# A linear-attention and gated-FFN kernel on one core: another way of bringing in the first weights and heads of k, and another order of the steps

## The chip, the core and the metric

The kernel runs on one core of a Trainium2 chip. It drives five engines that each take their instructions in order: TensorE (PE; its weight loads are listed apart as PEld), VectorE (DVE), ScalarE (ACT), GpSimd (POOL) and SyncE (SP). Transfers between memory and the core are started by SP, ACT or POOL and carried out by 16 DMA engines. The metric is the device time of one execution in microseconds; the median of several runs is given, with the lowest and highest.

## The reference

Attention with a feature map in place of the softmax, on 8 batches of 8 heads, 576 tokens and 64 dimensions, and a gated FFN on its output:

```python
def phi(x):                                    # w_phi: 64 x 128
    proj = np.einsum('bhsd,df->bhsf', x, w_phi)
    proj = proj - np.max(np.abs(proj), axis=-1, keepdims=True)
    return np.concatenate([np.exp(proj), np.exp(-proj)], axis=-1)
q_p, k_p = (phi(q), phi(k))
kv = np.einsum('bhsf,bhsd->bhfd', k_p, v)
z = np.sum(k_p, axis=2)
num = np.einsum('bhsf,bhfd->bhsd', q_p, kv)
den = np.einsum('bhsf,bhf->bhs', q_p, z)[..., None] + 1e-06
x = (num / den)                                # then 4608 tokens x 512
out = (np.maximum(x @ w_gate, 0.0) * (x @ w_val)) @ w_out   # 512 -> 1536 -> 512
```

## The kernel before

Everything is written as small steps, and one string, ORDER (from line 16), lists all 2041 of them in the order in which they are issued. Each word is a step: `ke.0.1.2.0:3@kp0` calls `do_ke` with the arguments 0, 1, 2, 0 (batch 0, head group 1, chunk 2, sign 0), the PSUM bank 3, and buffer 0 of the ring kp. The engines take their own instructions from this list in order, so a step that waits holds back all later steps of its engine. Waits between engines follow from the tiles that are read and written; there are eight PSUM banks.

Each batch has heads in three groups (0 and 1; 2 to 4; 5 to 7) and four chunks of 128 tokens, and 64 more tokens per head apart. The steps that matter here:

- Loads. `lk` (k, line 417), `lq` (q, line 424), `lm` (the 64 last tokens of k, lines 431 and 436), `lv` of batch 0 (v, line 454), `wl` (w_gate and w_val, line 477) and `wo` go by POOL, which casts fp32 to bf16 on the way where the tile is bf16. `wp` (line 373) and `wq` (line 379) bring w_phi in fp32 by SP: w32f holds four copies on 32 partitions each, w64f two copies on 64. `lv` of later batches (line 459), `lw` (the last tokens of v, line 469) and `gt` (line 466, one element of k read into a tile `mark`, behind which the next loads of SP wait until k has landed) go by SP.
- `wc` and `wd` cast w32f and w64f to bf16 on DVE (lines 382, 385). `ms` are memsets on DVE, `id` and `if` the identity on POOL and its fp32 copy on DVE.
- `zz.n` are n matmuls of zeros with zeros into a bank (line 408): filler that computes nothing.
- k of batch 0: `k0` transposes a head group on PE (line 533), `k1` copies it to kT on DVE (line 536), `k2` projects it with w64 (line 554). Later batches use `kt` (a DVE transpose, line 495) and `kr` (projection with w32, line 511). Then `ke` takes exponentials on ACT (line 563), `kx` maxima on DVE (line 571), `kk` and `kp` the scale factors on ACT (lines 580, 591), and `vs`, `vd`, `vr`, `vo`, `vp` scale v with them on POOL (lines 618, 637, 630) and DVE (lines 600, 608). `kv` multiplies features with v on PE (line 658), `kc` or `kd` copies it out (line 669).
- q: `qt` transposes on DVE (line 685), `qs` or `qc` projects with w32 on PE (line 694), `qe` exponentials on ACT (line 709), `qx` maxima on DVE (line 717), `qy`, `qz`, `qu`, `qw` the scale (lines 727, 735, 743, 750). `nu` multiplies with kv on PE (line 757); `nt`, `nv`, `nr` combine on DVE (lines 778, 788, 796); `nx` normalizes on POOL (line 800); `xp` with `xa` or `xc`, or a DMA transpose `xt` (line 817), puts the result into xT.
- FFN: group g takes the tokens of batch g, group 8 the last tokens of all. `fv` and `fg` (line 916; in group 0 partly by quarters, `pv` and `pg`, line 945) fill a bank, `va` (ACT, line 931) or `vb` (DVE, line 934) copies the value half out, `ga` (DVE, line 937) gates; `fo` (line 977) multiplies with w_out, `oc` (ACT) or `oe` (DVE) copies out, `od` stores by SP. The very last tile is done in two halves (`fp`, `o1`, `o2`, `d1` by ACT, `d2` by SP).

xT of group 8 has a tile of its own, xTm (`xT_mix`), 128 x 4 x 512 bf16, which is first written by the transposes of group 8, the first of them after the last tokens of batches 0 and 1 are done.

Of the kernel before, what the change touches and what calls it, by code (L numbers as in the profile page):

```python
# [8 lines left out]
FP32 = mybir.dt.float32  # L9
# [12 lines left out]
qt.0.0@qT1 kx.0.2.3:7 ke.0.2.2.1:6 kx.0.2.2:6 kx.0.0.0:2@mk2 lv.0.1 ke.0.0.2.1:1@kp2 ke.0.2.1.0:5  # L22
lm.1.0 lv.0.0 ke.0.0.3.1:3 ke.0.0.1.0:0 ke.0.2.0.0:4 lv.0.2 ke.0.0.0.1:2 kk.0.1.0 lm.1.1 wl.1.0
kx.0.2.1:5 kp.0.2.1:7 ke.0.0.0.0:2 ke.0.2.0.1:4 lw.0.1 qs.0.1.0:6 kx.0.0.1:0 kx.0.0.3:3 qx.0.1.0:6
vs.0.1.1@vs0 kp.0.2.0:7 qs.0.0.1:5 qe.0.0.1.0:5@qp0 gt.0 lk.1.3 qs.0.0.2:2 lv.1.2 kx.0.0.2:1
ke.0.2.3.0:7 vp.2:7@vs1 kk.0.0.1@ek1 vs.0.1.0 ke.0.0.2.0:1 qs.0.0.0:4 wl.0.1 kk.0.0.0 ke.0.0.3.0:3
qx.0.0.0:4 qx.0.0.2:2 vo.0@vs2 vd.0.2.0:7 ke.0.0.1.1:0 qs.0.1.1:1 qe.0.0.1.1:5 qe.0.0.0.1:4@qp1
qx.0.1.1:1 qs.0.1.2:3 qe.0.1.2.0:3@qp2 qe.0.0.0.0:4 qs.0.0.3:0 qe.0.0.3.0:0@qp3 wl.0.0 qe.0.1.0.0:6
qs.0.1.3:4 qx.0.0.1:5 qe.0.0.3.1:0 vd.0.2.1:7 qe.0.1.0.1:6 qe.0.1.1.0:1 vr.0.0.0 vr.0.0.1 qy.0.0:5
qx.0.1.2:3 vr.0.1.0 qx.0.1.3:4 vr.0.1.1 kv.0.2:7 kc.0.2:7@kv0 vo.1 kv.0.1:6 qz.0.0:5@my0 qu.0.0@mz0  # L30
qw.0.0@cq0 qx.0.0.3:0 kt.1.1@kT0 nu.0.0.2:7 nt.0.0.2:7@t0 qe.0.1.3.1:4 qy.0.1:0 qz.0.1:0@my0
vs.0.0.1 kc.0.1:6 ku.1@kT1 vs.0.0.0 kv.0.0:5 qe.0.1.3.0:4 nu.0.0.1:6 nt.0.0.1:6@t1 kc.0.0:5
qe.0.0.2.0:2 qu.0.1@mz0 qw.0.1 qy.0.2:0 qe.0.1.1.1:1 nv.0.0.1:6@u0 qe.0.1.2.1:3 qy.0.3:4 nu.0.0.0:5
nt.0.0.0:5@t2 qe.0.0.2.1:2 nv.0.0.2:7 nv.0.0.0:5 nr.0.0@r0 nu.0.1.1:1 qz.0.2:0@my0 qu.0.2@mz0 lv.1.0
# [12 lines left out]
qe.1.1.1.0:4 kr.1.0:2573 ke.1.0.1.1:5@kp0 ke.1.0.3.1:3 ke.1.0.2.1:7 ke.1.0.0.0:2 ke.1.0.3.0:3
pv.1.2:4 qt.1.0@qT0 kx.1.0.1:5@mk2 lw.1.1 pa.1.2:4@val1 ke.1.0.0.1:2 nx.0.3@xu1 xp.0.3:6 xc.0.3:6
kx.1.0.2:7 wl.1.2 pg.1.2:0 pb.1.0:1 ke.1.0.2.0:7 ke.1.0.1.0:5 kx.1.0.3:3 pv.0.3:6 pa.0.3:6@val0
fv.0.8:4 va.0.8:4@val2 ln.0.1 qc.1.0:5371 wo.2 pv.1.3:6 vs.1.1.0 kx.1.0.0:2 kk.1.0.0@ek0 kk.1.0.1  # L50
qe.1.0.1.1:3 vr.1.0.1 vs.1.0.0@vs0 pb.1.2:0 qx.1.0.2:7 qx.1.0.0:5 kt.1.2@kT1 qe.1.0.2.1:7
qe.1.0.3.0:1 qe.1.0.0.0:5 vr.1.1.0 qe.1.0.2.0:7 ms.1 pc.1.3:6@val1 pg.0.3:4 pb.0.3:4 qx.1.0.3:1
fv.0.10:0 va.0.10:0@val3 fv.0.11:2 lk.2.3 qe.1.0.0.1:5 va.0.11:2@val0 qx.1.0.1:3 kr.1.2:0476
kx.1.2.0:0@mk2 ke.1.2.3.0:6@kp1 pg.1.3:5 fg.0.11:2 kx.1.2.2:7 kx.1.2.3:6 qe.1.0.1.0:3 ke.1.2.1.1:4
kx.1.2.1:4 ke.1.2.2.0:7 qe.1.0.3.1:1 ku.2@kT1 ke.1.2.0.1:0 pb.1.3:5 kk.1.2.0@ek2 ke.1.2.2.1:7
fv.0.9:3 va.0.9:3@val1 fg.0.8:1 ke.1.2.1.0:4 wo.1 lv.2.3 ga.0.11:2 vr.1.0.0 qy.1.0:7 qz.1.0:7@my0
mt.0 fg.0.10:5 ga.0.8:1 kk.1.2.1 ke.1.2.0.0:0 vs.1.0.1 mc.0:4732 me.0.2.0:3 mx.0.3:2 me.0.0.0:4
qu.1.0@mz0 mx.0.2:3 me.0.0.1:4 vr.1.1.1 vo.1.0 kv.1.0:0 kc.1.0:0@kv1 ga.0.10:5 mx.0.0:4 qw.1.0@cq0
mx.0.1:7 vs.1.1.1 kv.1.1:1 me.0.2.1:3 kc.1.1:1 nu.1.1.0:0 nt.1.1.0:0@t2 fg.0.9:5 vo.1.2@vs1 lv.2.0
kt.2.1@kT0 vs.1.2.1 nu.1.0.0:1 me.0.3.1:2 ga.0.9:5 ke.1.2.3.1:6 nu.1.0.1:4 nu.1.1.1:3 nt.1.1.1:3@t0  # L60
nt.1.0.0:1@t1 vs.1.2.0 kv.1.2:6 nv.1.1.0:0@u0 nv.1.1.1:3 me.0.1.0:7 kt.2.0 lw.2.1 fo.0.1.0:5
kc.1.2:6 nu.1.0.2:6 nt.1.0.2:6@t0 nu.1.1.2:3 nt.1.0.1:4@t2 me.0.3.0:2 nu.1.2.0:2 nt.1.2.0:2@t3
nv.1.0.0:1@u1 me.0.1.1:7 lq.2.2 nv.1.0.2:6 nv.1.0.1:4 nr.1.0@r0 nv.1.2.0:2@u2 fo.0.1.1:5 fo.0.1.2:5
oc.0.1:5@ob0 nt.1.1.2:3@t2 nu.1.2.2:4 nt.1.2.2:4@t3 lw.2.0 nv.1.1.2:3 nr.1.1@r1 kr.2.0:2617
ke.2.0.0.0:2@kp0 kx.2.0.3:7@mk2 lv.2.1 ke.2.0.0.1:2 od.0.1 nu.1.2.1:0 nt.1.2.1:0@t2 nx.1.0@xu1
kx.2.0.2:1 ke.2.0.1.1:6 kx.2.0.0:2 nu.1.3.2:5 nt.1.3.2:5@t0 nv.1.2.1:0 ke.2.0.3.1:7 fo.0.0.0:3
fo.0.0.1:3 nv.1.3.2:5@u1 xt.1.0 fo.0.0.2:3 nu.1.3.0:5 ke.2.0.2.1:1 nv.1.2.2:4 nr.1.2@r0
nt.1.3.0:5@t3 nx.1.1@xu0 nu.1.3.1:0 nt.1.3.1:0@t0 nv.1.3.0:5 nv.1.3.1:0 nr.1.3@r1 ke.2.0.3.0:7
ke.2.0.2.0:1 oc.0.0:3@ob0 ke.2.0.1.0:6 kt.2.2@kT1 nx.1.2@xu2 kr.2.1:4172 ke.2.1.2.0:7@kp1 kx.2.0.1:6
fo.0.2.0:3 fo.0.2.1:3 ke.2.1.1.1:1 xt.1.1 ke.2.1.0.1:4 ke.2.1.3.1:2 fo.0.3.0:0 ke.2.1.0.0:4  # L70
# [190 lines left out]
def kernel(  # L261
# [17 lines left out]
    C = 4  # L279
# [787 lines left out]
```

## Time and profile before

| | |
|---|---|
| median of 3 runs | 378.97 us (378.84 to 379.15) |
| profiled execution | 378.79 us, of which the span of the profile is 376.8 us |
| PE busy | 367.3 us, 97% of the span |
| DVE busy | 296.3 us, 79% |
| ACT busy | 222.6 us, 59% |
| POOL busy | 161.4 us, 43% |
| memory read and written | 37.95 MB and 9.44 MB, 126 GB/s over the span |

A profile is one execution taken by the hardware profiler; its span is 2.0 us shorter than the time of that execution. Several views of it are used. The slices divide the span into 40 equal parts and give the busy share of each engine in tenths, and the granted clock of PE (PEclk) in tenths of full speed. The table of stages gives busy microseconds and the number of instructions of each engine in stretches that one chooses. The chain of waits follows the last instruction back, step by step, to what released it. The timeline lists instructions in order of time with the idle time before them. Matmul ends are modelled, so a busy PE is not yet a PE at its peak; the distance from one matmul's start to the next tells more.

### The profile page before, as it was taken

Reading aid. Unit: us, or ns where it says so; the run is one execution under the profiler, and the core shown is the slowest. Engines: PE = TensorE matmul, PEld = TensorE weight load, DVE = VectorE, ACT = ScalarE, POOL = GpSimd, SP = SyncE. Lnnn points to the kernel's source line nnn. Section 1 sums busy time; section 2 is a strip of 40 time slices with the busy share of each in tenths; the row PEclk is TensorE's granted clock in tenths of the full one; section 3 lists DMA queues with packets and bytes.
Section 4 is the critical chain, followed back from the end, with each engine's and each line's share of the span. In section 5 each row is a group of like instructions: output and inputs, shape, how many; then the busy total and the mean of one; then the engine's idle time right before and its main releaser. Section 6 shows DMA issues by size and latency. Waiting matters only on the chain.

```text
span 376.8 us, 9181 instructions
## 1 busy us (share of the span) xinstructions
PE 367.3 (97%) x3591; PEld 197.2 (52%) x3591; DVE 296.3 (79%) x680; ACT 222.6 (59%) x539; POOL 161.4 (43%) x180
## 2 busy tenths in 40 slices
PE   8788999999999999999999999999999999999996
PEld 6457857546544645455435554464444644444443
DVE  3989999989996899989989898888876657642351
ACT  1988996998578544776586547755774400302111
POOL 7777595595477042581475233812341212200000
PEclk9859999999999999999999999999999999999999
DMA  9999999699954664289713944193400021301122
GB/s 126 235 200 220 148 176 152 112 129 143 122 118 58 147 72 113 57 138 91 103 64 37 189 120 99 35 155 92 86 28 3 2 70 57 91 22 29 28 57 111
DMA packets 90513, 38.04 MB, mean 101 GB/s; under 512 B 64230, under 2 KB 85734, under 8 KB 90470
## 3 DMA queue, kind: packets, MB, share of 16 engines
q0 software_dynamic: 33904, 15.23, 31.2%
q1 hardware_dynamic: 56422, 22.10, 27.7%
q8 instruction: 28, 0.46, 0.6%
q10 hardware_dynamic: 144, 0.13, 0.1%
q14 instruction: 15, 0.12, 0.1%
HBM read 37.95 MB, written 9.44 MB: 126 GB/s over the span
## 4 chain that ended last, share of the span: by engine, by line
PE 89%; DVE 5%; ACT 4%; DMA 2%; issue 0%; SPq 0%; DVEq 0%; ACTq 0%
PE bank L916 46%; PE bank L977 22%; PE bank L658 6%; PE bank L757 4%; PE bank L945 4%; PE bank L694 3%; ACT kp L563 2%; PE bank L511 2%; DMA w64f<-in_w_phi_dram 2%; DVE mk L571 1%; ACT qp L709 1%; PE bank L1006 1%; PE bank L898 1%; DVE u L788 1%; DVE maxq L717 1%; DVE t L778 1%
## 5 line engine op out<-in xcount | busy, mean ns | idle before, releaser
L563 ACT ACTIVATE kp<-bank 128x384 bf16<-128x384 f32 x192 | 83.2, 513 | 26.2 <-PE bank L511 15.0
L977 PE MATMUL bank<-wo,h 128*128 128x512 bf16 x420 | 98.3, 379 | 0.0
L937 DVE SCALAR_TENSOR_TENSOR h<-bank,val 128x512 bf16<-128x512 f32 x100 | 66.3, 681 | 29.8 <-PE bank L916 25.5
L916 PE MATMUL bank<-xTs,wg 128*128 128x512 bf16 x352 | 86.7, 379 | 0.0
L916 PE MATMUL bank<-xTs,wv 128*128 128x512 bf16 x352 | 86.2, 379 | 0.0
L800 POOL TENSOR_TENSOR xu<-u,r 128x512 bf16<-128x512 f32 x36 | 37.5, 1044 | 97.3 <-DVE r L796 92.4
L931 ACT CAST val<-bank 128x512 bf16<-128x512 f32 x70 | 41.6, 606 | 62.2 <-PE bank L916 50.8
L709 ACT ACTIVATE qp<-bank 128x512 bf16<-128x512 f32 x128 | 70.9, 632 | 10.1 <-DVE maxq L717 5.1
L618 POOL TENSOR_TENSOR vs<-vn,ek 128x780 bf16<-128x780 f32 (+3 forms) x40 | 53.0, 1338 | 37.8 <-ACT ek L580 35.1
L977 PEld LDWEIGHTS <-h 128*128 128x128 bf16 x420 | 39.1, 98 | 44.0 <-issue 0.9
L916 PEld LDWEIGHTS <-wv 128*128 128x128 bf16 x400 | 37.0, 98 | 43.2 <-issue 3.5
L916 PEld LDWEIGHTS <-wg 128*128 128x128 bf16 x400 | 37.4, 98 | 42.0 <-issue 1.8
L571 DVE TENSOR_REDUCE mk<-bank 128x3 f32<-128x384 f32 x96 | 49.0, 539 | 4.3 <-ACT kp L563 2.2
L717 DVE TRANSPOSE_TENSOR_REDUCE maxq<-bank 128x16 f32<-128x512 f32 x64 | 42.3, 692 | 3.5 <-PE bank L694 2.3
L986 ACT COPY ob<-bank 128x512 f32<-128x512 f32 x23 | 13.6, 593 | 37.5 <-PE bank L977 37.2
L788 DVE TENSOR_TENSOR u<-bank,t 128x195 f32<-128x195 f32 (+1 forms) x108 | 33.4, 330 | 1.9
L778 DVE TENSOR_TENSOR t<-bank,cq 128x195 f32<-128x195 f32 (+1 forms) x96 | 29.8, 327 | 5.0 <-PE bank L757 4.1
L757 PEld LDWEIGHTS <-qp 128*128 128x128 bf16 x512 | 24.1, 98 | 13.6 <-issue 2.0
L757 PE MATMUL bank<-kv,qp 128*128 128x65 bf16 x512 | 27.2, 194 | 1.2 <-ACT qp L709 0.8
L934 DVE CAST val<-bank 128x512 bf16<-128x512 f32 x30 | 20.2, 678 | 8.4 <-PE bank L916 8.3
L658 PEld LDWEIGHTS <-kp 128*128 128x128 bf16 x640 | 24.0, 101 | 3.7 <-DVE h L937 0.3
L658 PE MATMUL bank<-vs,kp 128*128 128x65 bf16 x512 | 24.2, 199 | 0.0
(88 smaller groups left out, 357.0 us busy)
## 6 DMA issues: line engine op xcount, KB each, us to landing
out_dram<-ob SPq DMA_DIRECT2D x31, 256.0 KB, 2.2
vn<-in_v_dram SPq DMA_DIRECT2D x24, 256.0 KB, 5.4
kn<-in_k_dram POOLq DMA_DIRECT2D x7, 512.0 KB, 6.4
qn<-in_q_dram POOLq DMA_DIRECT2D x7, 512.0 KB, 7.6
wg<-in_moe_w_gate_dram POOLq DMA_DIRECT2D x3, 512.0 KB, 8.5
wv<-in_moe_w_val_dram POOLq DMA_DIRECT2D x3, 512.0 KB, 10.0
wo<-in_moe_w_out_dram POOLq DMA_DIRECT2D x3, 512.0 KB, 8.7
out_dram<-ob SPq DMA_DIRECT2D x9, 128.0 KB, 2.4
```

Of the source, the lines that this page charges most:

```text
L563: nc.scalar.activation(kp_of(3 * b + j)[:, i, s].rearrange("p n f -> p (n f)"), bank[bk[0]][:, 0 : 3 * F], AF.Exp, scale=(1.0, -1.0)[s],)
L571: nc.vector.tensor_reduce(mk_of(3 * b + j)[:, :, i], bank[bk[0]][:, 0 : 3 * F].rearrange("p (n f) -> p n f", f=F), axis=AX.X, op=ALU.max, ...
L618: nc.gpsimd.tensor_tensor(vs_of(3 * b + j)[:, s, 0:n].rearrange("p n i e -> p (n i) e")[:, :, 0:e], src[:, lo:hi].rearrange("p h i e -> p ...
L658: nc.tensor.matmul(out_ps[:, h - lo, s, :], lhsT=lhsT, rhs=rhs, start=(at == 0), stop=(at == 2 * n * (C + 1) - 1),)
L709: nc.scalar.activation(qp_of(4 * b + i)[:, s, 4 * hq : 4 * hq + 4].rearrange("p h m -> p (h m)"), bank[bk[0]], AF.Exp, scale=(1.0, -1.0)[s],)
L717: nc.vector.tensor_reduce(maxq[:, :, i, 4 * hq : 4 * hq + 4].rearrange("p t h -> p h t"), bank[bk[0]].rearrange("p (h t u) -> p h t u", h= ...
L757: nc.tensor.matmul(bank[bk[0]][:, E * n : E * (n + 1)], lhsT=qp_of(4 * b + i)[:, s, h, :], rhs=kv_of(b)[:, h, s, :],)
L800: eng.tensor_tensor(xu_of(n).rearrange("p (h d) -> p h d", d=D), u_of(n)[:, :, 0:D], r_of(n).to_broadcast([P, H, D]), op=ALU.mult,)
L916: nc.tensor.matmul(bank[bk[0]], lhsT=w[:, dc, P * f : P * f + P], rhs=xT(g)[:, dc, :], start=(dc == 0), stop=(dc == NDC - 1),)
L931: nc.scalar.copy(val_of(NFC * g + f), bank[bk[0]])
L937: nc.vector.scalar_tensor_tensor(h2_of(g, f), bank[bk[0]], 0.0, val_of(NFC * g + f), op0=ALU.max, op1=ALU.mult)
L977: nc.tensor.matmul(bank[bk[0]], lhsT=h2_of(g, f)[:, P * t : P * t + P], rhs=wo_sb[:, f, :], start=(f == 0), stop=(f == NFC - 1),)
```

## The change

The first load of k (heads 2 to 4 of batch 0, `lk.0.1`) is no longer done by POOL with a cast on the way. It goes by SP in fp32 (`lf`), as the first transfer of SP's queue, into the memory of xTm, seen as fp32; two casts then write bf16 k on chip, heads 2 and 3 on DVE (`cf.0`) and head 4 on ACT (`cg.1`). w_phi for 32 rows (`wp`) is second in SP's queue. w_phi for 64 rows is brought by ACT (`wr` in place of `wq`) as ACT's first instruction.

ORDER is another one throughout, with 2053 words. POOL now builds the identity first and then loads k of heads 5 to 7, k of heads 0 and 1, and q of heads 4 to 7. The filler is cut into 15 pieces (before 5): 16 matmuls on bank 0, then twelve pieces of 2 to 8 on bank 1, the last of them just ahead of `kv.0.2`, then 3 and 2 on bank 3 around the first `xp`; 79 filler matmuls in all (before 62). `wc` comes after the first maxima of k. Of the steps that may run on two engines, a few change: `oc` 22 and `oe` 13 (before 23 and 12), `va` 69 and `vb` 31 (before 70 and 30), `pa` 8 and `pc` none (before 7 and 1). All other kinds of steps are there as often as before.

```diff
 ORDER = """
-ms.0 ms.2 ms.3@vr0 lk.0.1 ms.6 wp wq ms.4@vr1 wd ms.5 lq.0.1 wc id if zz.37:0 k0.1:0 k1.1:0@kT0
-zz.5:1 k2.1:0123 lk.0.2 ke.0.1.1.0:1@kp0 ke.0.1.2.0:2 ke.0.1.3.0:3 ke.0.1.0.0:0 qt.0.1@qT0
-ke.0.1.3.1:3 kx.0.1.1:1@mk0 lk.0.0 kx.0.1.2:2 ke.0.1.2.1:2 ke.0.1.1.1:1 lm.0.1 zz.6:4 k0.2:4
-k1.2:4@kT0 zz.7:5 k2.2:4567 ke.0.2.2.0:6@kp1 kx.0.1.3:3 ke.0.2.3.1:7 lm.0.0 lq.0.0 kx.0.1.0:0
-kx.0.2.0:4@mk1 ke.0.1.0.1:0 lw.0.0 k0.0:2 k1.0:2@kT0 zz.7:1 k2.0:2013 kk.0.1.1@ek0 ke.0.2.1.1:5
...
-tail: fp.7.2.0:4 oc.7.3:6@ob2 od.7.3 o2.7.2:7@ob0 d2.7.2 o1.7.2:4 d1.7.2
+ms.0 ms.5 ms.4@vr0 id if lf wp ms.6 ms.2 wr cg.1 ms.3@vr1 cf.0 wd zz.16:0 k0.1:0 k1.1:0@kT0 zz.3:1
+k2.1:0234 ke.0.1.2.0:3@kp0 ke.0.1.3.1:4 lk.0.2 lk.0.0 kx.0.1.0:0@mk0 kx.0.1.1:2 ke.0.1.0.1:0 lq.0.1
+lm.0.0 lm.0.1 zz.3:1 k0.2:5 ke.0.1.0.0:0 lw.0.1 k1.2:5@kT0 gt.0 lw.0.0 lv.1.2 ke.0.1.1.1:2
+kx.0.1.3:4 ke.0.1.3.0:4 lv.0.1 zz.7:1 k2.2:5670 ke.0.2.2.0:7@kp1 ke.0.2.0.1:5 kx.0.1.2:3
+ke.0.1.1.0:2 lq.0.0 lm.1.1 lv.0.2 wc kk.0.1.1@ek0 kk.0.1.0 kx.0.2.1:6@mk1 kx.0.2.2:7 ke.0.2.1.1:6
+zz.6:1 k0.0:4 kx.0.2.0:5 ke.0.2.0.0:5 ke.0.2.2.1:7 kx.0.2.3:0 k1.0:4@kT0 zz.8:1 k2.0:4752
...
+tail: oc.7.3:7@ob0 fp.7.2.1:1 od.7.1 o2.7.2:1@ob2 d2.7.2 od.7.3 fp.7.2.0:7 o1.7.2:7 d1.7.2
 """
...
+    def do_wr(bk):
+        nc.scalar.dma_start(out=w64f, in_=w_phi[None].to_broadcast([2, D, F]))
...
+    def k_first():
+        flat = xT_mix.rearrange("p a b -> p (a b)").bitcast(FP32)[:, 0 : 3 * C * D]
+        return flat.rearrange("p (h x) -> p h x", h=3)
+
+    def do_lf(bk):
+        lo, hi = HEADS[1]
+        nc.sync.dma_start(
+            out=k_first().rearrange("p h (c d) -> p h c d", d=D),
+            in_=k[0, lo:hi, 0:SF, :].rearrange("h (p c) d -> p h c d", c=C),
+        )
+
+    def cast_first(copy, half):
+        lo, hi = ((0, 2), (2, 3))[half]
+        at = HEADS[1][0]
+        copy(
+            kn_of(0)[:, at + lo : at + hi].rearrange("p h c d -> p h (c d)"),
+            k_first()[:, lo:hi],
+        )
+
+    def do_cf(bk, half):
+        cast_first(nc.vector.tensor_copy, half)
+
+    def do_cg(bk, half):
+        cast_first(nc.scalar.copy, half)
```

(The two lines "tail" stand for the last words of each ORDER.)

More of the change, by code (lines that the diff above doesn't have):

```diff
@@ L23 @@
[L23 to L34, printed above, removed]
@@ L257 @@
+ga.7.3:7@hs10 fv.7.4:2 fo.7.3.0:7 fv.7.8:1 vb.7.8:1@val1 fg.7.8:6 ga.7.8:6@hs0 fo.7.0.0:3 fo.7.1.0:1
+od.8.3 va.7.4:2@val2 ga.7.4:0@hs1 fo.7.0.1:3 ga.7.11:5@hs3 fo.7.0.2:3 oe.7.0:3@ob2 fo.7.1.1:1
+fo.7.1.2:1 oe.7.1:1@ob1 od.7.0 fo.7.3.1:7 fo.7.3.2:7 oc.7.3:7@ob0 fp.7.2.1:1 od.7.1 o2.7.2:1@ob2
+d2.7.2 od.7.3 fp.7.2.0:7 o1.7.2:7 d1.7.2
 """
```

455 lines of the change are left out of this document (232 added, 223 removed).

## Prediction

> **What bounds the kernel now.** I read the page's slices first, then a table of stages, then the chain of waits over the first 34 us, then VectorE's timeline.
>
> The slices (9.4 us each):
>
> ```profile
> PE   8788999999999999999999999999999999999996
> DVE  3989999989996899989989898888876657642351
> PEclk9859999999999999999999999999999999999999
> ```
>
> The stages (columns: length; busy time and count for PE, PEld, DVE, ACT, POOL; granted clock, DMA share, GB/s):
>
> ```profile
> 0.00:8.00 8.00, 6.94 (x44) 5.18 (x45) 2.23 (x6) 1.28 (x1) 6.88 (x15) 1.00 0.78 118
> 8.00:16.00 8.00, 5.80 (x78) 3.96 (x76) 7.77 (x18) 6.28 (x18) 4.99 (x6) 1.00 1.25 239
> 16.00:27.00 11.00, 9.29 (x83) 4.87 (x82) 9.82 (x19) 9.72 (x28) 9.55 (x13) 0.53 1.25 196
> ...
> 32.00:72.00 40.00, 39.99 (x631) 29.04 (x628) 39.37 (x102) 34.93 (x89) 26.29 (x32) 1.00 1.11 165
> 72.00:204.00 132.00, 131.93 (x1304) 66.18 (x1301) 117.41 (x267) 93.71 (x228) 73.07 (x76) 1.00 0.64 99
> ```
>
> From 32 us on TensorE is never without work; only the first 32 us hold time that is not useful. Laid out by steps (a four-matmul FFN step starts 0.863 us after the last, a kv of three heads 0.95, a qc 0.56), the useful matmuls before the first FFN step at 32.16 add up to 11.0 us, so 21 us are filler (the zz matmuls on zeros, 10.7 us), half clock or waiting. The reader should also see VectorE: 39.37 of 40 us busy from 32 to 72. It is bound nearly as tightly as TensorE.
>
> What ends last in the start, from the chain:
>
> ```profile
> 1.56 6.35 DMA w64f<-in_w_phi_dram
> 7.91 0.02 issue
> 7.94 0.23 DVE w L385
> 8.16 0.14 DVE maxq L400
> 8.30 0.27 DVE w L382
> 8.57 0.13 DVE identf L391
> 8.70 0.48 DVE kT L536
> 9.18 0.05 issue
> 9.23 0.47 PE bank L554 x11
> 9.70 0.02 issue
> 9.72 3.95 ACT kp L563 x10
> ```
>
> The 64 KB copy of w_phi is waited for, not k: the first k load took 5.1 us from its issue at 1.25, so k was there by 6.4, w64f at 7.9. Three small VectorE steps then stand between w64f's cast and the first kT copy (8.62). From there VectorE runs to the first reciprocal (8.62 to 29.77, 21.15 us) with only 1.7 us of gaps (0.23, 0.31, 0.52, 0.46, 0.19).
>
> **The change, part by part.** Sums are made against the profiled execution (378.79 us, span 376.8); the median shown is 378.97, 0.18 above it, and the forecast is given on that scale.
>
> 1. *w64f by ScalarE's queue.* In SyncE's queue it stood behind w32f: the trace's packet records have w32f's rows from 2.27 to 4.34, w64f's from 4.59 to 7.55, landed at 7.91. So 3.3 us from first row to landing, beside POOL's loads. ScalarE issues first thing (its table load started at 0.73, now 0.4 to 0.6 later; ScalarE then waits anyway until 7 us, so that is free). SyncE's first issue at 0.74 had its first row at 2.27; the same gives 2.27 + 3.3 = 5.6. Upper bound: now three queues carry rows (k, then w32f; POOL's; this one) where it had one beside it, so 1.5 times 3.3, landing at 7.2. I take 5.6, because the row is this transfer's own.
>
> 2. *k of heads 2 to 4 in fp32 by SyncE.* No row for it. 384 rows of 1 KB; at w32f's pace (128 rows in 2.07 us) 6.2 us, landing at 8.8; at the 225 GB/s of the stage 27 to 32 us, 393 KB take 1.75 us, landing near 4.4. I take 4.4: that stage also moves v by SyncE in rows over all partitions. The casts: ScalarE's head, one copy of 256 columns, 0.40 us (the 128x256 ACTIVATE of line 853); VectorE's two heads 0.60 (128 columns 0.227, 256 columns 0.353, so 0.126 per 128 more). Both end near 5.1. Six transposes 0.34, to 0.7 if the clock is still half. So k stands in PSUM at 5.5 to 5.8, just before w64f is cast (5.85).
>
> 3. *VectorE's order.* The two memsets, identf and the maxq/maxm memsets now lie before the casts, in time in which VectorE waited 4.6 us for w64f: hidden, unless both loads come before 3.6 us. w32's cast (0.35) moves from before the first kT copy into the busy stretch: +0.35. First kT copy: 6.0 against 8.62, **-2.6**; with the cast **-2.25**.
>
> 4. *POOL's queue.* It loses one k load (0.93) and has the identity (0.54) first; k of heads 5 to 7 is issued at about 1.8 instead of 3.5, v of heads 2 to 4 at about 5.3 instead of 6.97. The q load of heads 4 to 7 goes from second to third, 2 us later, but its transpose moves behind the third kT copy. By the first k load's 5.1 us the second k lands at 6.9, by the later ones' 7.0 at 8.8. VectorE's second kT copy stands third in its queue, due at about 8.1: 0 to 1.1 us of wait, with all twelve maxima of k behind it. I take 0, as it is now the first of its queue. The mark DMA still holds SyncE's queue for k; the v loads behind it are needed only by batch 1.
>
> 5. *Filler on one bank.* 79 fillers in place of 62, spread on to the first FFN step; between the sixteen on bank 0 at the start and the five on bank 3 at the end all are on bank 1, which no step but the last few of the stage uses. They cannot wait on an eviction there. The half clock is what they can remove:
>
> ```profile
> 16.00:20.00 4.00, 3.23 (x10) 0.61 (x10) 3.69 (x9) 4.00 (x16) 3.41 (x5) 0.57 1.16 189
> 20.00:24.00 4.00, 3.06 (x21) 1.25 (x18) 3.48 (x6) 4.00 (x10) 3.84 (x8) 0.50 1.37 199
> 24.00:28.00 4.00, 4.00 (x86) 3.99 (x84) 3.43 (x9) 2.69 (x7) 2.30 (x3) 0.65 1.22 200
> ```
>
> kv.0.2 and kv.0.1 took 1.67 and 1.65 us there, 0.95 each later. That is 1.4 us on TensorE, of which VectorE's gaps show 1.17 (0.52, 0.46, 0.19). In the new order VectorE has 3.5 us of other work between the last vd and the first nt, so these gaps should close, but vr and vs on POOL (9.5 us in a row behind v's landing) may open one of the same size. I take 0 for both, bounds -1.7 (all gaps go) and +1.1 (point 4).
>
> TensorE: Matmul & The Clock Gate in the Trainium skill ("Part 1: The HAM clock gate") says that full clock comes after about 3.4 us of sustained work. 37 fillers took 6.60 us here (178 ns each) and seven later ones 0.93 (133 ns); sixteen are 2.8 us, so by that rule the first k projections may still be cold, at most 0.8 us (0.34 + 0.44 doubled) off the gain.
>
> 6. *The order after that.* I added the rows along both orders. VectorE's rows sum 6% above its busy time, hence a factor 0.94. From the first kT copy on, before's TensorE step is never earlier than VectorE's sum by more than 1.7 us until about 110 us, after which VectorE has slack. Where the useful matmuls reach 54 us, before has 71.4 us of VectorE rows ahead of it, the new order 73.6; at 60 us 76.7 and 79.3; at 66 they are equal. Before reached 54 at 76.2 us. The new sum gives 6.0 + 0.94 x 73.6 = 75.2, a gain of 1.0, or 2.7 with the 1.7 of lead seen elsewhere. Middle: 1.85. TensorE time lost there is not won back, since it is saturated to the end; later excesses (4.2 rows at 120 us) fall where VectorE has 8 us of slack. ScalarE has 3.6 us more at 60, against some 5 of slack. Three evictions change engine (one val, one ob, one pa): inside that sum. Tail: d2 now stands before od.7.3; d1's landing still ends it: 0 (-0.2 to +0.4).
>
> Sum: the smaller of 2.25 and 1.85, **-1.9**: 376.9 for a profiled execution, **377.1** on the median's scale.
>
> **The rivals.**
>
> - *All gaps close.* 2.25 + 1.7 = 3.95, and VectorE leads as far as it ever did: 375.0 to 376.2. For it: the clock row. Against: VectorE's sum at 54.
> - *The rows share.* If the engines serve three queues in turn, w64f lands at 7.2, the kT copy starts at 7.5, gain 1.1 - 0.35 = 0.75, less what point 6 takes: 0.2 to 0.8, near 378.4. For it: w64f's own pace beside one queue. Against: POOL's rows start only at about 3.4.
>  DMA: Bandwidth & Descriptors in the Trainium skill ("Issuing engines are not separate DMA queues") says that queues of different engines run on the same 16 DMA engines and interleave, so that a second issuer saves only issue time; by it this rival comes true, 0.6 us saved.
> - *w64f comes last* (slower). If SyncE's queue goes first, k's 393 KB (1.75 us, point 2) stand ahead of w32f and w64f: landing 7.91 + 1.75 = 9.65, kT copy at 9.95, 1.3 late, plus 0.35: 380.6. It decides from a landing later than 8.0. For it: in before w64f did wait for every row of w32f. Against: that was one queue.
> - *It does not do what it says*: k early, but the later order adds as much: 378.9.
>
> **How the numbers follow.** Forecast (gain 1.0 to 2.7) 0.49; gaps close 0.13; rows share 0.18; w64f last 0.15; nothing 0.05. What a measurement can tell from no change is 0.2%, 0.76 us. Faster: 0.49 + 0.13 and 0.04 of the sharing case, 0.66. Same: the rest of it and the last, 0.19. Slower: 0.15. The range 375.2 to 379.0 leaves out the slower case and the far end of closing gaps.
>
> **What would show it.** Right: VectorE's w64f cast near 5.9, first kT copy near 6.0, first exponential of k near 7.1, PEclk without a 5 in the third slice, first FFN matmul near 29 to 30, and about the same offset where TensorE has done 54 us. Wrong: a DMA wait on w64f, k or the second k ahead of VectorE past 7 us; TensorE idle between 60 and 90 us behind VectorE.

## The result and the profile after

The changed kernel takes **381.28 us** (median of 20 runs, 379.88 to 384.40) against 379.12 for the kernel before (20 runs, 378.21 to 380.32): ratio **1.0067** (95% interval 1.0053 to 1.0081). It is 2.2 us slower, where 1.9 us faster was forecast; it lies outside the range of 375.2 to 379.0. The profiled execution took 380.65 us, with a span of 378.9.

The start came as forecast. VectorE's first instructions in the changed kernel, from the timeline (start us, us, engine, line, operation, count, and the idle time before with what ended it):

```profile
4.39 0.43 DVE L441 CAST kn<-xTm 128x512 bf16<-128x512 f32 x1 [0.84 <-DMA xTm<-in_k_dram]
5.85 0.23 DVE L390 CAST w<-w64f 128x128 bf16<-128x128 f32 x1 [1.03 <-DMA w64f<-in_w_phi_dram]
6.00 0.55 DVE L566 COPY kT<-bank 128x768 bf16<-128x768 bf16 x1
```

k is cast at 4.39, w64f at 5.85 and the first kT copy starts at 6.00 instead of 8.62: 2.6 us won. The slices of the changed kernel:

```profile
PE   6898999999999999999999999999999999999996
DVE  5998999989998898989977987899577647541451
PEclk9999999999999999999999999999999999999999
```

The 5 in the third slice of PEclk is gone, and VectorE begins sooner. The table of stages of the changed kernel (same columns as before's) gives the amounts:

```profile
0.00:8.00 8.00, 5.38 (x40) 3.35 (x40) 4.42 (x12) 2.53 (x5) 6.61 (x14) 1.00 0.75 134
8.00:16.00 8.00, 6.37 (x70) 4.43 (x71) 6.04 (x14) 6.93 (x22) 5.74 (x7) 1.00 1.30 260
16.00:27.00 11.00, 9.89 (x139) 6.21 (x139) 10.96 (x23) 10.33 (x26) 9.10 (x13) 1.00 1.29 197
27.00:32.00 5.00, 3.77 (x74) 2.81 (x71) 4.72 (x22) 3.67 (x10) 1.90 (x2) 1.00 1.29 192
32.00:72.00 40.00, 39.21 (x627) 28.55 (x634) 37.27 (x97) 35.50 (x91) 25.77 (x32) 1.00 1.05 158
72.00:204.00 132.00, 129.79 (x1292) 65.55 (x1307) 117.42 (x266) 91.58 (x223) 73.46 (x77) 1.00 0.67 110
```

The granted clock is 1.00 from 16 to 27 us, where before had 0.53. VectorE is busy 37.27 of 40 us from 32 to 72 where it was 39.37, and TensorE idles 0.8 us there and up to 2.2 us from 72 to 204 (before 0.0 and 0.1). Not all of this is waiting: 49 of the 3608 matmuls have no record in this trace, and the waits from 72 to 204 us that name what ended them add up to 1.0 us. So TensorE now waits, and VectorE is not full there. For what it waits, its timeline and its waits tell:

```profile
31.27 1.96 PE L975 MATMUL bank<-xTs,wv 128*128 128x128 bf16 x32 [1.11 <-DMA wv<-in_moe_w_val_dram]
...
37.19 0.81 PE L724 MATMUL bank<-qT,w 32*128 32x512 bf16 x8 [0.43 <-DVE qT L715]
```

The first FFN matmul could have run at 30.16. It waits 1.11 us for a third of w_val that is still landing. The new order begins the FFN with the first third (`pv.0.0`), where before began with the second (`pv.1.0`); both issue the second third first. So the new order issues the third that it needs first behind the other, at 17.95; it lands at 31.22. At 37.19 the next wait is for q of batch 1, whose VectorE transpose waits for its load in turn. In its first 36 us, the chain of waits of the changed kernel has two loads (start us, us, what):

```profile
1.44 7.13 DMA kn<-in_k_dram
8.57 0.05 issue
8.61 0.52 PE bank L563 x6
9.14 0.02 issue
9.16 0.56 DVE kT L566
...
22.70 0.98 POOL vs L648
23.68 12.33 DMA qn<-in_q_dram
```

Where the chain of before had w64f and three VectorE steps, it now has the second k, 7.13 us from issue to landing; the second kT copy behind it starts at 9.16. The load of q takes 12.33 us, against 9.36 (25.35 to 34.71) in before. A later piece of the chain shows another load:

```profile
152.22 1.44 POOL vs L648
153.66 8.53 DMA kn<-in_k_dram
162.20 0.02 issue
162.22 0.38 DVE kT L525
...
162.98 0.59 DVE h L967
163.56 0.04 issue
163.61 1.12 PE bank L688 x30
```

k of batch 5 is issued at 153.66; before issued it at 129.80. Its transposes wait 1.20 us for it and stand in VectorE's queue ahead of an FFN gate that TensorE waits for (0.8 us in the waits of PE, the longest after 40 us).

To see where the time goes I took TensorE's steps of both kernels at the same amount of useful work done (P, in us of matmul rows, filler left out) and subtracted their times. One profiled execution each; negative is ahead of before. In e3's execution the granted clock fell in the first stage (section on the clock), in those of after, e7 and e8 it did not:

| P, us | 10 | 20 | 50 | 120 | 160 | 344 (end) |
|---|---|---|---|---|---|---|
| after | -2.5 | -0.1 | 0.0 | +0.2 | +1.35 | +1.8 |
| e3_weights_v | -0.4 | +0.4 | +0.3 | +0.7 | +1.3 | +1.8 |
| e7_repairs | -2.7 | -1.7 | -1.6 | -1.0 | -0.4 | -0.3 |
| e8_repairs_fill | -2.7 | -1.4 | -1.4 | -1.05 | -0.9 | -0.7 |
| e12_old_head | 0.0 | 0.0 | +1.4 | +1.7 | +2.3 | +2.2 |

After wins 2.5 us, has lost them where 20 us of work are done (about 42 us after the start), and loses 1.8 more from 50 on.

### The profile page after: what moved, and what is told of

Its sections match the earlier page's. It is cut to its first block, busy times and chain, and to the rows that moved or that the text cites. A ratio compares the mean times of both kernels' runs of the same rounds, so it can differ in the third digit from the quotient of the medians.

```text
span 378.9 us, 9168 instructions
## 1 busy us (share of the span) xinstructions
PE 364.0 (96%) x3559; PEld 195.8 (52%) x3608; DVE 295.5 (78%) x682; ACT 222.7 (59%) x539; POOL 160.3 (42%) x179
## 4 chain that ended last, share of the span: by engine, by line
PE 80%; DMA 8%; ACT 3%; issue 3%; DVE 3%; POOL 2%; SPq 0%; POOLq 0%; DVEq 0%; ACTq 0%
PE bank L946 42%; PE bank L1007 21%; PE bank L688 5%; DMA kn<-in_k_dram 4%; PE bank L787 4%; DMA qn<-in_q_dram 3%; PE bank L975 3%; PE bank L541 2%; PE bank L724 2%; ACT kp L593 2%; POOL vs L648 1%; DMA out_dram<-ob 1%; PE bank L1036 1%; POOL vr L667 1%; DVE qT L715 1%
## 5 line engine op out<-in xcount | busy, mean ns | idle before, releaser
L1007 PE MATMUL bank<-wo,h 128*128 128x512 bf16 x406 | 95.8, 379 | 1.2 <-issue 0.3
L593 ACT ACTIVATE kp<-bank 128x384 bf16<-128x384 f32 x192 | 81.4, 510 | 19.9 <-PE bank L541 11.8
L946 PE MATMUL bank<-xTs,wg 128*128 128x512 bf16 x337 | 85.1, 379 | 0.9 <-issue 0.2
L946 PE MATMUL bank<-xTs,wv 128*128 128x512 bf16 x334 | 84.1, 379 | 1.3 <-ACT qp L739 0.2
L961 ACT CAST val<-bank 128x512 bf16<-128x512 f32 x69 | 40.5, 594 | 59.5 <-PE bank L946 55.2
L946 PEld LDWEIGHTS <-wg 128*128 128x128 bf16 x400 | 36.6, 97 | 41.4 <-issue 2.1
L964 DVE CAST val<-bank 128x512 bf16<-128x512 f32 x31 | 21.1, 683 | 10.4 <-PE bank L946 9.0
L688 PEld LDWEIGHTS <-kp 128*128 128x128 bf16 x640 | 22.4, 98 | 4.2 <-DVE h L967 1.3
L688 PE MATMUL bank<-vs,kp 128*128 128x65 bf16 x512 | 23.0, 194 | 0.9 <-DVE h L967 0.8
## 6 DMA issues: line engine op xcount, KB each, us to landing
wg<-in_moe_w_gate_dram POOLq DMA_DIRECT2D x3, 512.0 KB, 10.7
```

Of the source, the lines that this page charges most:

```text
L593: nc.scalar.activation(kp_of(3 * b + j)[:, i, s].rearrange("p n f -> p (n f)"), bank[bk[0]][:, 0 : 3 * F], AF.Exp, scale=(1.0, -1.0)[s],)
L688: nc.tensor.matmul(out_ps[:, h - lo, s, :], lhsT=lhsT, rhs=rhs, start=(at == 0), stop=(at == 2 * n * (C + 1) - 1),)
L946: nc.tensor.matmul(bank[bk[0]], lhsT=w[:, dc, P * f : P * f + P], rhs=xT(g)[:, dc, :], start=(dc == 0), stop=(dc == NDC - 1),)
L961: nc.scalar.copy(val_of(NFC * g + f), bank[bk[0]])
L1007: nc.tensor.matmul(bank[bk[0]], lhsT=h2_of(g, f)[:, P * t : P * t + P], rhs=wo_sb[:, f, :], start=(f == 0), stop=(f == NFC - 1),)
```

## The experiments

The theory after the result: the loads between 4 and 36 us, and the places where they are issued, take the early start back; then the late k of batch 5 and other waits of the new order make it slower. The rivals: the clock (fillers now stand on TensorE's own path, and the clock may fall), and an order whose later part costs time wherever it starts. All kernels compute the whole reference; times are compared with runs of before on the same chip.

**The two halves, and the weights.** The first kernel is before with the new loads and casts and before's order; the second is the new order with before's loads.

```diff
 (e1_front_alone: before's ORDER)
-lk.0.1 ms.6 wp wq ms.4@vr1 wd ms.5 lq.0.1 wc id if zz.37:0 ... lk.0.2
+lf ms.6 wp wr cg.1 ms.4@vr1 ms.5 id if lk.0.2 lq.0.1 cf.0 wd zz.16:0
 (and wc ahead of zz.7)
 (e2_order_alone: after's ORDER)
-ms.4@vr0 id if lf wp ms.6 ms.2 wr cg.1 ms.3@vr1 cf.0 wd zz.16:0
+ms.4@vr0 lk.0.1 id if wp ms.6 ms.2 wq ms.3@vr1 wd zz.37:0
```

> The order of before, with the new front alone: k of heads 2 to 4 in fp32 first in SyncE's queue, the two casts, w64f by ScalarE, 16 fillers, GpSimd's other loads one place earlier, w32's cast after the second kT copy. My theory, that the front is a gain and the new order gives it back: first exponentials near 7.2 us instead of 9.72, and at least 1 us of that kept to the end, 376.5 to 378.0 us where before has 379.1, since this order's own waits for loads are only 0.2 us in all. The rival, that the front itself costs (more bytes in the first 6 us, so that q, v and the weights land later, and the later loads take the lead back whatever the order): 378.8 us or more.

> The new order with the old front: k of heads 2 to 4 by GpSimd with its cast, w64f by SyncE, 37 fillers. My theory (the order loses about 2 us in the first stage and 1.5 us after it): first exponentials back at 9.7 us, the first FFN matmul not much later than in the changed kernel (31.3 us), because it waits for w_val there and not for the chain; 381 to 382 us. If the order were sound and the front the loss, it would be at or below before, 377 to 379 us.

Measured: e1 380.95 against 378.55, **1.0061** (1.0047 to 1.0075); e2 381.47, **1.0083** (1.0063 to 1.0103). Neither half gains, and the two losses do not add up to that of the whole (1.0067). The early start by itself is worth less than nothing in the old order. VectorE in e1_front_alone:

```profile
10.48 1.08 DVE L713 STREAM_TRANSPOSE qT<-qn 128x512 f32<-128x512 f32 x1 [3.91 <-DMA qn<-in_q_dram]
11.42 0.95 DVE L599 TENSOR_REDUCE mk<-bank 128x3 f32<-128x384 f32 x2
12.30 0.54 DVE L564 COPY kT<-bank 128x768 bf16<-128x768 bf16 x1
```

VectorE stands 3.91 us at the transpose of q, with the second kT copy queued behind it, and TensorE waits 2.90 us for that copy; the offset is +1.9 from there to the end. The old order fits the old landings; e6, below, fits it to the new ones.

```diff
 (e3_weights_v: after's ORDER)
-wl.0.1 ... wl.0.0
+wl.0.0 ... wl.0.1
 (and lv.1.3 behind lw.1.0 instead of some words earlier)
 (e4_k5_early: after's ORDER; lk.5.3 moved)
+lk.5.3 vs.4.0.0
-lk.5.3 (63 words later)
```

> The changed kernel with two repairs of the loads: the first third of w_val (used first) is issued where the second was, and the second where the first was; of v of batch 1 one quarter more (256 KB) goes behind the wait of SyncE for the last tokens, as in before. My theory: TensorE's wait of 1.1 us for w_val at 31.3 us goes, the q of batch 1 lands about 1 us before its 36.0 us, and 0.7 to 1.8 us of the end time go: 379.5 to 380.6 us beside 381.3 of the changed kernel. Rival, the loss comes from how the order places VectorE's and ScalarE's work: within 0.3 us of the changed kernel.

> The changed kernel with one repair: k of batch 5 is issued by GpSimd ahead of the first scaling of v of batch 4 (about 140 us) and not behind the third (153.66 us). My theory: VectorE's wait of 1.2 us for it at 162 us and TensorE's of 0.8 us behind it go, and 0.7 to 1.2 us of the end time: 380.1 to 380.6 us. Rival, the next late thing (the other engines' work at that place) takes it: within 0.3 us of the changed kernel's 381.3.

Measured: e3 379.57 against 378.55, **1.0031** (1.0018 to 1.0044): exchanging the two thirds of w_val and moving one load of v in the issue order takes half of the loss away. The first FFN step of e3 no longer waits for w_val. e4 384.35, **1.0150** (1.0135 to 1.0164): a miss. POOL in e4_k5_early:

```profile
146.40 0.96 POOL L422 DMA_DIRECT2D kn<-in_k_dram  x1 [5.68 <-DVE kT L525]
```

The load was put so early that its buffer was still being read; POOL stood 5.68 us with everything behind it. It says nothing against the theory, but shows what a load that is issued too early costs: 3 us more than after.

**Fillers, and the repairs.**

```diff
 (e5_no_fillers: after's ORDER)
-every zz but zz.16:0
 (e6_front_fitted: e1's order, and)
-qt.0.1 behind the first exponentials; wc ahead of zz.7
+qt.0.1 behind the third kT copy; wc behind the first four maxima of k
-zz.6:4 zz.7:5
+zz.11:4 zz.4:5
 (e7_repairs: e3's ORDER; lk.5.3 some 40 words earlier, ahead of nx.3.3)
-od.8.2 ... od.8.0
+od.8.0 od.8.2
 (e8_repairs_fill: e7's ORDER)
-zz.3:1 ahead of k0.2; zz.7:1 ahead of k2.2
+zz.10:1; zz.3:1
```

> The changed kernel without its fillers behind the first 16 (it computes the same; 63 matmuls of zeros are left out). In two runs of the new order with the new front (the two repairs of the first batch) the granted clock fell to 0.5 from 8.8 us on, the seven fillers ahead of the second projection took 1.70 us in place of 0.93, and the projection came 0.8 us later, although its kT copy was done. Theory A, the fillers stand in TensorE's own way: without them the second projection follows the kT copy at 9.7 to 9.9 us at either clock, the stage to 28 us is not longer than in those runs, and the time is that of the changed kernel or up to 0.5 us less (380.8 to 381.3), since w_val's landing at 31 us takes up what the start gains. Theory B, the fillers hold the clock and that is worth more: the clock is 0.5 from about 8 to 28 us, numerator and kv matmuls take twice as long, and the time is 0.5 to 2 us more (381.8 to 383.3).

> The order of before with the new front, as in the front alone, but with the order fitted to it in four places: the first transpose of q goes behind the third kT copy (q lands at 10.4 us, and VectorE stood 3.9 us before it), w32's cast stands behind the first maxima, 11 fillers in place of 6 ahead of the second transposes and 4 in place of 7 behind them. Theory A, the front alone lost only because steps in fixed order now wait for loads that land no earlier: VectorE's wait of 3.9 us goes, the clock stays up, and the time is 376.8 to 378.3 us, below before (378.6). Theory B, the loads of the first stage are the bound (k of heads 5 to 7 at 8.6 us, q at 10.4, v at 13 to 15, all engines of the DMA full): the lead shrinks to under 0.5 us at the first v scaling, 378.3 to 379.5 us.

> The changed kernel with the two repairs of the loads of the first batch (379.6 us), and two more: k of batch 5 is issued at about 146 us, right after the k buffer is read for the last time, not at 140 (where GpSimd stood 5.7 us before it, with all that is queued behind) nor at 153.7; and the store of tile 0 of group 8 goes ahead of that of tile 2, whose copy frees its output buffer. Theory: TensorE's wait of 0.6 to 1.2 us at 162 us and of 0.3 us at 358 us go: 378.6 to 379.0 us, level with before. Rival, the late wait of 162 us is taken by another (GpSimd's scalings of v of batch 4 come 1 us later): 379.3 to 380 us.

> The four repairs, and the fillers moved from the place where they hold up TensorE to where it idles: 10 in place of 3 ahead of the second transposes (idle from 7.5 to 8.5 us), 3 in place of 7 behind them. Theory A: the clock holds through the wait for the second k in every run, the second projection comes 0.1 to 0.8 us earlier, and 0 to 0.8 us less than with the repairs alone: 378.0 to 378.9 us, with less spread. Theory B (w_val or q of batch 1 sets the end of the first stage whatever the start does): within 0.2 us of the repairs alone.

Measured, against 379.08 (381.28 is after's, beside 379.12): e5 382.77, **1.0104** (1.0083 to 1.0124), above after's whole interval, so the fillers together help more than they cost; e6 378.95, **0.9993** (0.9983 to 1.0002), so e1's loss is gone and nothing is gained; e7 379.33, **1.0008** (0.9992 to 1.0024); e8 379.60, **1.0021** (1.0000 to 1.0042). e7, four places of issue away from after, has lost the loss, but is no faster than before: 378.6 to 379.0 was expected, 379.3 to 380 if another wait took the place of the one for batch 5. Moving the fillers (e8) gave nothing that these runs can tell. TensorE of e7 at the place where after waited:

```profile
29.10 0.84 PE L541 MATMUL bank<-w,kT 32*128 32x128 bf16 x24
29.88 1.96 PE L975 MATMUL bank<-xTs,wv 128*128 128x128 bf16 x32
31.67 0.29 PE L787 MATMUL bank<-kv,qp 128*128 128x65 bf16 x4
```

Here the first FFN step starts at 29.88 and waits for nothing: the forecast had said 29 to 30. q lands at 34.4 instead of 36.0, and at P = 20 the kernel is 1.7 us ahead, 1.6 more than after, the 1.11 + 0.43 us of after's two waits. The wait for batch 5 is gone too. One of 0.66 us stands at 75.16, at the first FFN step of group 1, put down to an exponential; after has 0.25 us there. Of e7's 2.7 us at P = 10, 0.3 are left at the end. What the k load and the store give by themselves was not run apart from each other; e3's and e7's intervals overlap.

**Is it the later part of the order?** The first kernels keep the repaired order for the first stage and go over to before's sequence at about 36, 54 and 71 us; the fourth has before's first 359 words and then the repaired order.

```diff
 (e9_splice_36, e10_splice_54, e11_splice_71)
+e8's words up to the seam, then before's remaining words in before's order
 (e12_old_head)
+before's first 359 words, then the remaining words in e8's order
```

> All of the work, in a spliced order: the first 242 words of the order with the four repairs and the fillers moved (to about 36 us), then what is left in the sequence of before, with PSUM banks and buffers taken anew where they are not yet free. With that front TensorE is 1.4 to 1.7 us ahead of before after 20 us of useful work. Theory A, the new front and first stage are a gain, and the new order loses it later (0.6 to 1.5 us between 20 and 344 us of useful work, at many small places): 377.0 to 378.0 us where before has 379.1, the first version below both. Theory B, before's sequence fits only its own start, and the lead is lost at its next wait for a load: 378.6 to 379.6 us.

> The same with the splice at about 54 us (368 words of the repaired new order, then before's sequence). The lead there is 1.5 to 1.9 us in the profiles. Theory A: 377.0 to 377.8 us. Theory B, as above: 378.6 to 379.6 us.

> The same with the splice at about 71 us (503 words of the repaired new order). The lead there is 1.4 to 1.6 us; some 0.5 us is lost in the new order by 80 us. Theory A: 377.2 to 378.2 us. Theory B: 378.6 to 379.6 us.

> The other way about: the front and the order of before for its first 359 words (to about 56 us), then what is left in the sequence of the new order with its repairs. If the later part of the new order loses time by itself, as theory A has it, this is slower than before by the 0.6 to 1.5 us that the repaired kernels lose after 20 us of useful work: 379.7 to 380.6 us. If the later part is sound and only the start decides, it is within 0.3 us of before (379.1).

Measured, against 379.22: e9 386.00, **1.0163** (1.0140 to 1.0185); e10 381.90, **1.0074** (1.0051 to 1.0098); e11 382.49, **1.0089** (1.0058 to 1.0119); e12 381.47, **1.0057** (1.0038 to 1.0075). The three splices lose at the seam and lie above both of their expectations, so they do not tell what the early start would be worth without one; e10 keeps 1.5 us ahead up to P = 34 and is 2.08 behind from 50 to the end, with nothing lost after. That before's later part loses nothing, and the new one from P = 50 to the end 0.7 us (e8) or 0.8 (e12, both in the table) to 1.8 (after), is what they show. e12's own +1.4 at P = 50 is lost at its seam.

**Is it the clock?** The mean granted clock of each run gives a first answer without an experiment (the kernel before, run beside them, had medians of 379.12, 378.55, 379.08, 379.08 and 379.53, its clock always below 0.994):

| | runs at 0.994 or more | their median | runs below | their median |
|---|---|---|---|---|
| after | 10 | 380.65 | 10 | 382.47 |
| e3_weights_v | 7 | 379.44 | 2 | 381.02 |
| e7_repairs | 8 | 378.97 | 4 | 380.76 |
| e8_repairs_fill | 8 | 379.00 | 4 | 380.94 |
| e15_more_fill | 11 | 380.00 | 1 | 382.07 |

In half of after's runs the clock falls, and these are 1.8 us longer; but those with full clock are still 1.5 us above before's 379.12, and from after to e7 both groups fall by 1.7. So full clock and shorter runs go together in these five kernels, and the places of issue move both groups. In e5_no_fillers they do not go together: its two runs at 0.994 or more took 382.96 and 384.51, and the four below have a median of 382.6. TensorE in after, profiled at full clock:

```profile
8.61 0.51 PE L563 MATMUL bank<-ident,kn 128*128 128x128 bf16 x6 [1.07 <-DMA kn<-in_k_dram]
8.96 0.93 PE L413 MATMUL bank<-zero 128*128 128x256 bf16 x7
9.82 0.51 PE L584 MATMUL bank<-w,kT 64*128 64x128 bf16 x12
```

and in e3_weights_v, the same words up to there, profiled in a run in which it fell:

```profile
8.51 0.72 PE L563 MATMUL bank<-ident,kn 128*128 128x128 bf16 x6 [1.11 <-DMA kn<-in_k_dram]
9.02 1.70 PE L413 MATMUL bank<-zero 128*128 128x256 bf16 x7
10.65 0.82 PE L584 MATMUL bank<-w,kT 64*128 64x128 bf16 x12
```

The seven fillers ahead of the second projection take 1.70 us instead of 0.93, and the projection starts 0.83 later: at a granted clock of 0.50 (9 to 12 us in e3) a filler on the path costs 1.8 times as much. The Trainium skill, TensorE: Matmul & The Clock Gate ("Part 1: The HAM clock gate"), says that the clock falls after an idle window of about 3.4 us, counted in windows that run freely. Here it fell, in some runs and not in others, with no idle stretch longer than that wait of 1.1 us ahead of it; the run-to-run change agrees with free windows, the length does not.

```diff
 (e13_clock_held: before's ORDER; e14_front_clock: e6's)
+zh.22:0 behind k2.0; zh.8:7 and zh.16:7 some 50 words later
 (zh: fillers of 96 columns, into columns that no other step uses)
 (e15_more_fill: e8's ORDER)
-zz.3:1 ... zz.8:1 ... zz.7:1
+zz.8:1 ... zz.14:1 ... zz.13:1
 (e16_k2_first: e15's ORDER)
-id if ... lk.0.2
+lk.0.2 id if
```

> Before, with 46 more fillers of 96 columns into columns 416 to 511 of a bank whose other columns hold projections (unused by the kernel): 22 behind the third k projection, 8 and 16 ahead of two of q's. They cover the waits of TensorE at 14.2, 18.8 and 21.1 us after which the granted clock was 0.5 until 26.6 us. Theory A, the half clock is on the path (kv of heads 5 to 7 took 3.3 us at it, 1.9 us at full): 377.6 to 378.6 us beside 379.1. Theory B, ScalarE's exponentials and GpSimd's scalings bound that stage whatever TensorE's clock: 378.9 to 379.5 us.

> The front fitted into the order of before (378.95 us), with the same 46 fillers. Theory A: 0.7 to 1.5 us less than without them, 377.4 to 378.3 us, below before. Theory B: 378.7 to 379.3 us.

> The four repairs with the fillers moved (378.2 to 382.7 us, median 379.6; clock 0.985 to 1.0), with 17 more fillers on the zero bank: 8 in place of 3 ahead of the first projection, 14 in place of 8 ahead of the third, 13 in place of 7 ahead of the first q of heads 0 to 3. Theory A, its slow runs are those in which the clock fell, and the waits of TensorE at 5.6, 12.3 and 15.6 us let it fall: all runs at a clock of 0.997 or more, 378.2 to 379.0 us, spread under 1 us. Theory B, the clock falls for another reason: the same spread as without.

> As the one with more fillers, and GpSimd issues k of heads 5 to 7 before it builds the identity: issue at 0.7 in place of 1.4 us. Theory A, that landing holds the stage: the second transposes start at 7.8 to 8.1 us in place of 8.4, and 0.2 to 0.5 us less at the end. Theory B, the transfer shares the DMA engines with the fp32 k and lands when those bytes are through: landing and time the same within 0.2 us. The identity comes 0.9 us later (2.2 us), still ahead of its first use at 4.8.

Measured, against 379.53: e13 382.57, **1.0083** (1.0055 to 1.0111), and e14 381.39, **1.0064** (1.0039 to 1.0089). Both are inconclusive on the clock, for the fillers brought a wait of their own, in e13_clock_held:

```profile
21.34 0.82 PE L409 MATMUL bank<-zero 128*128 128x96 bf16 x8 [2.64 <-ACT qp L716]
```

Though they write columns that no other step uses, the eight waited 2.64 us for ScalarE's exponentials from that bank, and the clock was 0.50 from 21 to 30 us, so it was not held. e15 380.10, **1.0022** (1.0007 to 1.0037): the clock is full in 11 of 12 runs, and its median at full clock is 1.0 us above that of e8. But before, run beside it, was 0.45 us slower as well (379.53 for 379.08), and of the 1.2 us by which e15's profiled execution is behind e8's some 0.5 are lost by P = 50 and some 0.7 behind it, where a wait of 0.82 us at 76.05 (0.32 in e8) is put down to a DMA transpose of x. So seventeen more fillers go with a clock that holds, and the time is not better; what they cost on TensorE's own path is not told apart. e16 380.02, **1.0018** (1.0002 to 1.0034): the second k was issued first, but only 0.19 us earlier (0.7 was expected), and landed at 8.7 in both.

**The front in the old order, fitted further.**

```diff
 (e17_vector_fit: e6's ORDER; kx.0.1.3 ahead of the second kT copy,)
-k1.0:2@kT0 qt.0.1@qT0
+qt.0.1@qT0 ahead of kx.0.2.0
 (e18_vector_fit2: e17's ORDER)
-qt.0.0@qT1 kx.0.2.3:7 ke.0.2.2.1:6 kx.0.2.2:6
+kx.0.2.3:7 ke.0.2.2.1:6 kx.0.2.2:6 qt.0.0@qT1
```

> The front fitted into before's order (378.95 us, 0.9993 of before) with two VectorE steps moved: the third maximum of k ahead of the second kT copy (VectorE idles from 8.4 to 9.05 us), the first transpose of q ahead of the maximum and the third kT copy (q has landed at 10.2, VectorE idles 0.7 us before that copy). Theory A, VectorE's row holds the stage: its six maxima end at 16.0 to 16.5 us in place of 17.0 and 0.3 to 0.8 us are kept to the end: 378.1 to 378.7 us, below before. Theory B, landings (v of heads 2 to 4 near 13.9 us, q) hold it: 378.8 to 379.1 us.

> As the one before, and the second transpose of q (1.0 us) behind three of the six maxima, so that the bank of q's first projection is free about 1 us earlier. Theory A: 0.2 to 0.5 us less than without, 377.8 to 378.4 us. Theory B, the second half of q is then late for its own projections: the same or 0.3 us more.

Measured, against 379.27: e17 378.80, **0.9991** (0.9979 to 1.0002); e18 378.65, **0.9985** (0.9974 to 0.9996), the only version whose interval lies below 1, by 0.6 us of the 2.6 by which its front is earlier. The chain of waits of e17_vector_fit says what takes the rest (its first lines after 4 us):

```profile
3.86 1.21 POOL km L459 x2
5.07 7.74 DMA qn<-in_q_dram
12.81 0.03 issue
12.84 1.08 DVE qT L713
...
14.19 2.40 DVE mk L599 x5
```

The q load, issued at 5.07 where before issued it at 6.23, lands at 12.81; before's landed at 13.14. In e18 the chain starts with a load that takes 7.18 us, of the last tokens of k. By TensorE's steps e17 is 2.1 us ahead at P = 1 and 0.8 at P = 3. The early start runs into loads that land hardly earlier. e17 (378.80) came out as expected if landings hold the stage (378.8 to 379.1); e18 against e17 is within the noise.

## Why the prediction was wrong, step by step

1. *w64f by ScalarE's queue:* right in the number, with luck. Forecast 5.6 (bound 7.2); its cast starts at 5.85. But its first row came at 3.70 and not at 2.27, and its rows took 1.8 us (to 5.50) where 3.3 to the landing were counted: the two errors cancel.
2. *k in fp32:* right. Forecast 4.4; the first cast starts at 4.39 and takes 0.43 (0.60 was counted).
3. *VectorE's order:* right in place, 6.00 for 6.0. The net 2.25 shows as 2.5 at P = 10, but by luck: 1.1 us went to the second k (point 4), and the full clock, counted at 0 (point 5), made up for it. In e3's profiled execution, whose clock fell, the same front is only 0.4 ahead there.
4. *POOL's queue:* the bound came true, not the value. The second k was taken to land at 6.9 and landed at 8.57 (bound 8.8). TensorE waits 1.07 us, and the second kT copy starts at 9.16 where 8.1 was needed: +1.1 where 0 was taken. "It is now the first of its queue" was no reason: from issue to landing it took 7.13 us, not the 5.1 of the first k load of before. In e16, issued 0.19 us earlier still, it landed no earlier.
5. *Filler on one bank:* half right. In the profiled execution the clock is full all through, but in half of the runs it falls. The first projections were not slow: twelve take 0.51 us at 6.60 and at 9.82. A term of 1.8 us that only some runs have was counted at 0, with the cost of fillers on TensorE's own path.
6. *The order after that:* **the step that failed.** Its sum followed VectorE's rows to P = 54 (75.2 us forecast, some 76.2 reached) and had no load behind the first stage in it. VectorE was not what TensorE waited for longest there: VectorE has 2.7 us free between 32 and 72, while TensorE waits 1.11 us for w_val (at 31.27) and 0.43 for q (at 37.19). The DMA share was in the table that I showed: in the second and third stage the packets took 1.25 times the engines' time in before, and 1.32 from 27 to 32 us; in after it is 1.30, 1.29 and 1.29. Loads issued earlier there landed later: k of batch 1 (14.74 for 16.58) at 24.50 for 23.90, the first third of w_val (17.95 for 19.90) at 31.22 for 29.89, q (23.68 for 25.35) at 36.02 for 34.71. In the first stage the second k (issued at 1.44 for 3.51) and the first v (5.09 for 6.97) had landed as much earlier as they were issued (8.57 for 10.62, 12.24 for 14.14). e7, which changes places of issue alone, shows that these places cost 1.6 of the 2.4 us lost between P = 10 and 20.

   The sign named for VectorE, TensorE idle behind it between 60 and 90 us, did not come (0.25 us there, put down to ScalarE); that of a DMA wait on the second k past 7 us did. "TensorE is saturated to the end" failed too: 1.8 us are lost after P = 50, with k of batch 5 behind the largest single wait (0.8 us). From P = 160 to the end after loses 0.45 and e7, which exchanges two stores of group 8, 0.1. The rest is in waits of 0.25 us and below, and stays open. So does why e7, with all four places repaired, still gives back 2.4 of its 2.7 us.

**The rivals.** "The rows share" and "w64f comes last" both needed w64f after 7 us: it was there by 5.85, so they fell. The Trainium skill, DMA: Bandwidth & Descriptors ("Issuing engines are not separate DMA queues"), says that a second issuer saves only the time of issue. For w64f it saved 2 us (7.91 to 5.85 or less): its rows, no longer behind w32f's in one queue, started 0.9 us earlier (3.70 for 4.59) and took 1.1 us less. What the rule says of sharing is not told apart here: SP's queue had moved 1.47 MB by 28 us instead of 0.94 and POOL's 4.22 by 30 us instead of 4.35, but 0.33 MB of the one and 0.20 of the other are the first k and w64f, which changed queues. (The rows of POOL's first load, which the first of these rivals put at about 3.4, start at 2.90 in before's trace.) "All gaps close" was half right: VectorE is busy 10.96 of 11 us from 16 to 27, and what that gave was gone by P = 20. "It does not do what it says" came nearest, at 0.05, with 4.3 us lost behind the front (from -2.5 to +1.8) where it allowed for some 2. None of the rivals had the mechanism that decided.

**What stays open.** How much of the lead a later part without losses would keep: every splice lost more at its seam. And how much of the spread of after's runs the clock itself makes: the runs go together with it, but no kernel held it without adding work.

## What to carry to other kernels

Before an early start is credited to the end, list every load that is needed in the next 30 us with its issue and its landing, and ask of each whether it lands earlier: here the second k and the first v, issued 2 us earlier, landed 2 us earlier, and three loads issued 1.7 to 2 us earlier between 14 and 24 us landed 0.6 to 1.3 us later, and the lead shrank at the first of these three that TensorE waited for. An order that is moved against its loads has to be fitted again place by place; one load behind the wrong neighbour held TensorE for 1.1 us here, and one that waited for its buffer held POOL for 5.7 and cost 3.

## What the runs showed of the hardware

- The time of a load depends on what else is under way. The same five loads of 512 KB (a third of w_gate, k of batch 1, the second and the first third of w_val, q of batch 1) took 8.5, 7.3, 7.6, 10.0 and 9.4 us in before and 10.7, 9.8, 8.5, 13.3 and 12.3 in after, at a DMA share of 1.2 to 1.3. The last third of w_val, issued at 36.25 in after, where the share has fallen to 0.81 (36 to 44 us), took 5.6. By 28 us all queues together had moved 5.56 MB in after and 5.26 in before, 0.2 of the difference being the first k in fp32. That the bytes ahead of a load set its landing is argued from this, not tested.
- POOL held its ninth load until its first had landed, though they share no tile. POOL in the changed kernel:

```profile
6.63 0.72 POOL L466 DMA_DIRECT2D km<-in_k_dram  x1
8.86 1.58 POOL L484 DMA_DIRECT2D vn<-in_v_dram  x2 [1.51 <-DMA kn<-in_k_dram]
11.05 0.76 POOL L507 DMA_DIRECT2D wv<-in_moe_w_val_dram  x1 [0.62 <-DMA qn<-in_q_dram]
```

 The load of v waits 1.51 us for k, that of w_val 0.62 for q; before shows the same, 0.50 us at its load of v at 10.91. That eight loads may be on their way at a time is read from these lines and was not tested, nor whether the chip or the program's own waits set it.
- The same words took two courses in the first 12 us: where the granted clock stayed at 1.00 (after) a filler took 133 ns, where it fell to 0.50 behind a 1.1 us wait (e3) 243.
